# Second q in quarters, heads 7-6 and 5-4 first, then heads 3-0 as one half, and the place of half a V tile

## The chip, the cores and the metric

The kernel runs on one core of one Trainium2 chip. The metric is the device time of one execution in microseconds. It was measured three times for the kernel before: 178.45, 178.59 and 178.68 us, median 178.59 us. One further execution was profiled, and every duration below is from it.

## The reference

Four rows of 512 numbers pass through an attention layer A, a gated layer B, and then through both again with the same weights:

```python
x = x + _A_ref(_layernorm(x), A_k_cache, A_v_cache, A_wq, A_wo)
x = x + _B_ref(_layernorm(x), B_w_gate, B_w_up, B_w_down)
x = x + _A_ref(_layernorm(x), A_k_cache, A_v_cache, A_wq, A_wo)
x = x + _B_ref(_layernorm(x), B_w_gate, B_w_up, B_w_down)
```

In A, q is `x @ wq` (512 x 4096) for 4 rows and 32 heads of 128. The last 2048 positions of the K and V caches are used, in 8 key-value heads, each shared by 4 query heads. Scores are scaled and go through a softmax, the weighted V are multiplied by wo (4096 x 512). B is `(sigmoid(x @ w_gate) * (x @ w_up)) @ w_down` with 1792 hidden columns. All tensors are bf16. K and V of the window are 16 MB each, wq and wo 4 MB each, and the three matrices of B about 1.8 MB each.

## The kernel before, in words

All weights and caches come from HBM by transfers that SP issues (`dma`, line 398) into one SBUF arena of 50 slots of 128 x 2048 bf16 (0.5 MB each). K of all eight heads stays in the first 32 slots, four slots a head; the rest is a pool of pairs of slots. A program of operations is built first (`_Plan.op`), each with what it reads and writes; `_schedule` (line 92) then orders the operations of each engine by estimated times, and `_assign_sync` gives each the semaphore waits that its dependencies need. SP's order is the order of building; after `P.chain = True` TensorE's is too. A transfer whose place is still being read waits on SP, and everything behind it on SP waits as well.

Around the second attention there is too little room, so pieces of the arena are used in halves. `homes` gives the slots to which a half is bound: Y, Z and GA are the places of the V tiles V(7,0), V(7,1) and V(6,0) (head, pair of batches), GB is a free pair, and a number 0 or 1 says which of its two slots. `hfree` lists the ones that are free. `load_glu(0)` puts the first B's weights there, `load_wq(1)` (line 522) the second q's weights: eight transfers of 0.5 MB, first the four of heads 7 to 4 (i = 1), one for each 128 of the 512 inputs, then the four of heads 3 to 0 (i = 0). `load_v` (line 609) loads V(6,0) and V(5,1) of the second attention in halves.

V(7,0) and half of V(7,1) of the first attention are needed again in the second and are not loaded twice. `stash` and `stash_half` transpose them into PSUM banks (0 to 3, and 4 and 5), and they return later: `load_stash` (line 587) writes banks 0 to 3 into a pair from the pool, `unstash_half` (line 603) writes banks 4 and 5 back into slot Z.

The second attention goes through heads 7 to 0 (u = 0 to 7). In `q_second` (line 824) TensorE multiplies heads 7 to 4 into bank 6; VectorE transposes it (`q_turn`, line 803) into `qh`. `q_unit` (line 834) spreads one head of q over a block-diagonal operand, `softmax_unit` (line 861) makes the mask product M and the scores S and then, in `soft`, the maximum and the exponential, `turn_p` transposes the weights, `pv_wide` multiplies by V. `attn_second` (line 1201) writes this order out by hand. When the scores of a head are done, its K slots go to the pool, and `fill` puts the next transfers on SP. The banks of scores are given by the line

```python
bank, pt = {HKV: (OBS[0], 2), HKV + 1: (WB, 3)}.get(u, (SB[k2], k2))
```

so head 7's scores go to bank 4, head 6's to bank 6, later ones to banks 0 and 1.

## Time and profile before

| | |
|---|---|
| median of three runs | 178.59 us |
| profiled execution: its time, its span | 178.86 us, 177.1 us |
| mean granted TensorE clock | 0.944 |
| busy: TensorE products, VectorE, ScalarE | 102.2, 104.4, 32.7 us |
| DMA | 70.52 MB, 12882 packets, mean 398 GB/s |
| V: loads, size, median time to landing | 27 of 1024 KB, 22.6 us, and 3 of 512 KB, 5.6 us |
| second wq: loads, size, median time to landing | 8 of 512 KB, 6.1 us |

The span runs from the first to the last instruction. A share of busy time is an average over stages. The granted clock is 1.0 in each 2 us slice from 92 to 156 us and 0.5 from 158 us on. The time from issue to landing says how deep the DMA queue is when a transfer is put in: 6.1 us around the second q, over 20 us for most others. In the views shown below, a line of the timeline holds start and duration in us, engine, source line and operation, and in brackets how long the engine had been idle and what ended that; a line of the slices holds the stretch, its length, the busy time of the five engines, TensorE's clock, the DMA share and GB/s; a line of the chain holds start, duration and what.

### The profile page before, as it was taken

Reading aid. Unit: us, or ns where it says so; the run is one execution under the profiler, and the core shown is the slowest. Engines: PE = TensorE matmul, PEld = TensorE weight load, DVE = VectorE, ACT = ScalarE, POOL = GpSimd, SP = SyncE. Lnnn points to the kernel's source line nnn. Section 1 sums busy time; section 2 is a strip of 40 time slices with the busy share of each in tenths; the row PEclk is TensorE's granted clock in tenths of the full one; section 3 lists DMA queues with packets and bytes.
Section 4 is the critical chain, followed back from the end, with each engine's and each line's share of the span. In section 5 each row is a group of like instructions: output and inputs, shape, how many; then the busy total and the mean of one; then the engine's idle time right before and its main releaser. Section 6 shows DMA issues by size and latency. Waiting matters only on the chain.

```text
span 177.1 us, 3893 instructions
## 1 busy us (share of the span) xinstructions
PE 102.2 (58%) x1641; PEld 55.0 (31%) x1653; DVE 104.4 (59%) x256; ACT 32.7 (18%) x87; POOL 21.6 (12%) x88
## 2 busy tenths in 40 slices
PE   0536336481842635607417866466986999776664
PEld 0202102241431421603404752052322444435322
DVE  7307997838476374593483772323299999742351
ACT  2002031312030300300201101000043455430011
POOL 6100010101010100100100100000011453342000
PEclk9999999999999999999999999999999999975555
DMA  5999999999999999999999999999999999999980
GB/s 182 425 427 424 429 420 416 407 425 429 411 413 417 425 422 418 407 422 431 413 416 429 401 402 405 401 408 381 407 416 411 420 420 424 418 411 406 413 347 24
DMA packets 12882, 70.52 MB, mean 398 GB/s; under 512 B 1336, under 2 KB 1344, under 8 KB 6720
## 3 DMA queue, kind: packets, MB, share of 16 engines
q1 hardware_dynamic: 12856, 70.26, 97.2%
q8 instruction: 13, 0.21, 0.5%
q14 instruction: 5, 0.04, 0.1%
q10 hardware_dynamic: 8, 0.00, 0.0%
HBM read 70.26 MB, written 0.00 MB: 397 GB/s over the span
## 4 chain that ended last, share of the span: by engine, by line
DMA 38%; DVE 32%; PE 18%; issue 4%; SPq 4%; ACT 3%; DVEq 0%; ACTq 0%
DMA arena<-in_B_w_down_dram 15%; DMA arena<-in_A_v_cache_dram 15%; DVE arena L854 11%; PE ps L883 7%; DVE nmax L896 5%; DMA arena<-in_B_w_gate_dram 4%; DMA arena<-in_A_wq_dram 4%; SPq L398 4%; PE ps L973 3%; PE ps L872 2%; DVE nmax L900 2%; DVE mxt L904 2%; DVE ebuf L931 2%; PE ps L1162 2%; DVE arena L1064 2%
## 5 line engine op out<-in xcount | busy, mean ns | idle before, releaser
L854 DVE STREAM_TRANSPOSE arena<-arena 128x1024 f32<-128x1024 f32 x32 | 37.0, 1202 | 0.0
L883 PE MATMUL ps<-arena,qbd 128*32 128x512 bf16 x256 | 25.5, 534 | 0.0
L896 DVE TENSOR_REDUCE nmax<-ps 128x1 f32<-128x512 f32 x16 | 10.8, 676 | 19.4 <-PE ps L883 19.2
L973 PE MATMUL ps<-ebuf,arena 128*128 128x8 bf16 x576 | 17.8, 168 | 7.6 <-DMA arena<-in_A_v_cache_dram 4.2
L872 PE MATMUL ps<-msk_m,msk_s 128*32 128x512 bf16 x64 | 8.6, 526 | 23.1 <-DVE arena L854 21.8
L973 PEld LDWEIGHTS ps<-ebuf,arena 128*128 128x128 bf16 x576 | 16.8, 104 | 9.6 <-DMA arena<-in_A_v_cache_dram 5.5
L911 ACT ACTIVATE prow<-ps,nmax 128x512 bf16<-128x512 f32 x16 | 11.0, 687 | 35.1 <-DVE nmax L908 29.5
L847 ACT CAST qbd<-ps 128x256 bf16<-128x256 f32 x16 | 5.9, 370 | 44.9 <-PE ps L883 35.0
L940 POOL CAST s<-psm 128x1 bf16<-128x1 f32 x9 | 1.7, 187 | 83.9 <-ACT prow L911 83.9
L883 PEld LDWEIGHTS ps<-arena,qbd 128*32 128x32 bf16 x256 | 8.3, 121 | 10.4 <-issue 7.8
L795 PE MATMUL ps<-arena,xn 128*4 128x512 bf16 x64 | 8.3, 572 | 5.0 <-DMA arena<-in_A_wq_dram 4.5
L926 ACT CAST prow<-ps 128x512 bf16<-128x512 f32 x16 | 9.4, 586 | 9.8 <-PE ps L973 2.1
L1342 PE MATMUL ps<-arena,xn 128*4 128x448 bf16 x64 | 7.8, 548 | 4.1 <-DMA arena<-in_B_w_up_dram 1.9
L931 DVE STREAM_TRANSPOSE ebuf<-prow 128x256 f32<-128x256 f32 x16 | 7.0, 436 | 3.8 <-ACT prow L926 3.7
L872 PEld LDWEIGHTS ps<-msk_m,msk_s 128*32 128x32 bf16 x64 | 1.7, 98 | 24.1 <-DVE arena L854 22.7
L773 ACT ACTIVATE lnv<-ps 128x4 f32<-128x4 f32 x4 | 0.7, 174 | 41.0 <-PE ps L769 41.0
L807 DVE STREAM_TRANSPOSE ebuf<-ps 128x512 f32<-128x512 f32 x3 | 2.1, 717 | 10.2 <-PE ps L795 10.1
L1055 PE MATMUL ps<-arena,ebuf 128*32 128x512 bf16 x112 | 8.0, 409 | 0.2 <-DVE nmax L908 0.2
L842 PE MATMUL ps<-qh,eyew 32*128 32x64 bf16 x64 | 5.6, 217 | 3.8 <-ACT qbd L847 2.4
L1351 DVE STREAM_TRANSPOSE ebuf<-ps 128x448 f32<-128x448 f32 x4 | 2.6, 650 | 7.0 <-PE ps L1342 7.0
L1162 PE MATMUL ps<-onp,arena 128*128 128x16 bf16 x144 | 5.3, 175 | 2.5 <-DVE onp L996 2.2
L981 DVE TENSOR_TENSOR onb<-ps,rinv 128x16 bf16<-128x16 f32 x9 | 1.7, 185 | 8.3 <-PE ps L973 8.1
(112 smaller groups left out, 132.2 us busy)
## 6 DMA issues: line engine op xcount, KB each, us to landing
arena<-in_A_v_cache_dram SPq DMA_DIRECT2D x27, 1024.0 KB, 22.6
arena<-in_A_k_cache_dram SPq DMA_DIRECT2D x16, 1024.0 KB, 25.2
arena<-in_A_wq_dram SPq DMA_DIRECT2D x4, 1024.0 KB, 7.9
arena<-in_A_wq_dram SPq DMA_DIRECT2D x8, 512.0 KB, 6.1
arena<-in_A_wo_dram SPq DMA_DIRECT2D x3, 1024.0 KB, 26.2
arena<-in_B_w_down_dram SPq DMA_DIRECT2D x4, 512.0 KB, 6.3
arena<-in_B_w_gate_dram SPq DMA_DIRECT2D x4, 448.0 KB, 8.4
arena<-in_B_w_up_dram SPq DMA_DIRECT2D x4, 448.0 KB, 6.1
```

The lines of the kernel that those rows point to most:

```text
L795: last = pe.matmul(ps[32 * hh:32 * hh + NB, qb, :], xn[:, c * NB:(c + 1) * NB], src[:, o + hh * 512:o + (hh + 1) * 512], start=(c == 0), s ...
L854: P.op("vector", "T%d_%d" % (h, t), c_dve(1024), lambda v, v32=v32: v.transpose(v32, v32), r=[("slot", 4 * h + t)], w=[("slot", 4 * h + t)])
L872: last = pe.matmul(ps[32 * gi:32 * gi + 32, bank, :], msk_s[:, :], msk_m[:, :].unsqueeze(1).broadcast_to([128, 256, 2]), start=True, stop= ...
L883: last = pe.matmul(ps[32 * gi:32 * gi + 32, bank, :], qbd[:, q0:q0 + 32], kt[:, cp // 2, cp % 2, jh * NJ:(jh + 1) * NJ, :], start=False, s ...
L896: lambda v: v.tensor_reduce(nmax[:, k2:k2 + 1], ps[:, bank, :], AXX, ALU.max),
L911: lambda a: a.activation(prow[:, :].rearrange("p (m x t) -> p m x t", x=32, t=2), ps[:, bank, :].rearrange("p (m t x) -> p m x t", x=32, t ...
L926: P.op("scalar", "pc" + tag, c_act(512), lambda a: a.copy(prow[:, :], ps[:, pb, :]), r=[("ppb", pb)], w=[("prow",)], banks=(pb,))
L931: P.op("vector", "pt" + tag, c_dve(256), lambda v: v.transpose(et, prow[:, :].bitcast(F32)), r=[("prow",)], w=[("e", k2)])
L973: last = pe.matmul(ps[:, ob, bp * 8:bp * 8 + 8], src[:, j * 128:(j + 1) * 128], ev[:, j % 2, j % 16 // 2, x0:x0 + 8], start=(j == 0), stop ...
L1055: last = pe.matmul(ps[32 * g:32 * g + 32, ob, :], ew[:, g, mq, t], src.rearrange("p (m t d) -> p t m d", t=2, d=128)[:, t], start=(n == 0) ...
L1162: last = pe.matmul(ps[:, WB, c * NR:(c + 1) * NR], tile_ap(s)[:, o + r_ * D + c * 128:o + r_ * D + (c + 1) * 128], ov[:, r_ * NR:(r_ + 1) ...
L1342: last = pe.matmul(ps[32 * g:32 * g + NB, gub[n], 0:NF], xn[:, c * NB:(c + 1) * NB], slot_ap(s)[:, g * NF:(g + 1) * NF], start=(c == 0), s ...
```

## The change

The weights of heads 7 to 4 still come in four transfers of 0.5 MB, but each now holds two of the four blocks of 128 inputs and the columns of two heads: 128 partitions of 2 rows of 1024 columns. The pair for heads 7 and 6 comes first (j = 1), then that for heads 5 and 4. `q_pair` multiplies them with 256-wide products, two for each group of columns, into bank 6 and into columns 256 to 511 of bank 7, and `q_pair_turn` transposes each quarter and multiplies by the reciprocal deviation, twice, with a factor that is zero on the rows of the other head (`hide`, two more exponentials). Heads 3 to 0 come last as before, but their second block goes to the first slot of Z, and all four products are made after head 6's scores, into bank 4. Head 7's scores go to bank 6, head 6's to bank 5.

The half tile returns from banks 4 and 5 into the first K slot of head 7 (`base[KA]`), one half before head 7's maximum and one after its `nm`; the second of those slots takes the second half of V(5,1), whose first half goes to Y; V(6,0)'s half goes to GA. The first pair of head 7's K slots therefore reaches the pool later. `load_stash` comes after the third load of V instead of the second. On SP, V(4,0) waits for the third scores of the second attention, where it had waited for the second.

On the engines this makes 16 more products and weight loads on TensorE, six more instructions on VectorE, two more on ScalarE; SP issues the same number of transfers.

```diff
-        msks = sb("msks", [128, 22], F32)
+        msks = sb("msks", [128, 24], F32)
...
-        selm = msks[:, 18:22].bitcast(BF16)
+        selm, hide = msks[:, 18:22].bitcast(BF16), msks[:, 22:24]
...
+        BACK = ("back",)
+        KA = ("first",)
...
             def emit(s):
-                dma(str(name), slot_ap(s)[:, 0:size], src, w=[("slot", s)], rate=rate)
+                dst = slot_ap(s)[:, 0:size]
+                if name[0] == "wqp":
+                    dst = dst.rearrange("p (f n) -> p f n", f=2)
+                dma(str(name), dst, src, w=[("slot", s)], rate=rate)
             loads.append((name, emit))
...
             else:
-                for i in (1, 0):
-                    for c in range(NC):
-                        load_half(("wq", c, k, i), wq_d[:, c, i * SLOT:(i + 1) * SLOT], "bw_4k", SLOT,
-                                  (((Y, 1), (GB, 0), (GB, 1), (GA, 0)), ((GB, 0), (GB, 1), (GA, 0), (Y, 0)))[i][c])
+                for j in (1, 0):
+                    for n in range(2):
+                        o = SLOT + j * (SLOT // 2)
+                        load_half(("wqp", n, j), wq_d[:, 2 * n:2 * n + 2, o:o + SLOT // 2], "bw_4k", SLOT,
+                                  (((GA, 0), (Y, 0)), ((GB, 0), (GB, 1)))[j][n])
+                for c in range(NC):
+                    load_half(("wq", c, k, 0), wq_d[:, c, 0:SLOT], "bw_4k", SLOT, ((Y, 1), (Z, 0), (GB, 0), (GB, 1))[c])
...
 
-        def unstash_half(after):
-            for n in range(2):
-                dst = slot_ap(base[Z])[:, n * 1024:(n + 1) * 1024].bitcast(F32)
+        def unstash_half():
+            where[BACK] = base[KA]
+            left[BACK] = 1
+            halves[HKV - 1, 1] = [(BACK, 0), (Z, 1)]
+            for n in (1, 0):
+                dst = slot_ap(base[KA])[:, n * 1024:(n + 1) * 1024].bitcast(F32)
                 P.op("vector", "uo%d" % n, c_dve(512), lambda v, dst=dst, n=n: v.transpose(dst, ps[:, OBS[n], :]),
-                     r=[("so", n)], w=[("slot", base[Z])], banks=(OBS[n],), after=after)
+                     r=[("so", n)], w=[("slot", base[KA])], banks=(OBS[n],))
 
...
             name = ("V", h, bp, k)
-            tiles = {(HKV - 2, 0): ((Y, 0),), (HKV - 3, 1): ((Y, 1), (GB, 0))}.get((h, bp)) if k else None
+            tiles = {(HKV - 2, 0): ((GA, 0),), (HKV - 3, 1): ((Y, 0), (KA, 1))}.get((h, bp)) if k else None
             if tiles is not None:
...
                     halves[h, bp].append((half, 0))
+                    if tile == (KA, 1):
+                        on_free[half] = lambda s: pool.release(s - 1)
                 if len(tiles) == 1:
...
+        on_free[BACK] = lambda s: None
...
+        P.op("vector", "zero_c", 300.0, lambda v: v.memset(ps[:, CB, 256:512], 0.0), w=[("c0",)], banks=(CB,))
...
+        P.op("vector", "hide", 100.0, lambda v: v.tensor_scalar(hide[:, :], maskb[:, :], 1.0, 1.0e30, ALU.subtract, ALU.mult),
+             r=[("maskb",)], w=[("hide",)])
...
                      r=[("cb",)], w=[("lnv",)], banks=(CB,))
+                if tag == "Q":
+                    for n, (rs, t) in enumerate(((lnd[:, 0:nb], ("lnd",)), (lnr[:, NB:NB + nb], ("lnr", 1)))):
+                        P.op("scalar", "ln_rs%d" % n, c_act(NB),
+                             lambda a, n=n, rs=rs: a.activation(rs, lnv[:, 0:nb], ACTF.Exp, bias=hide[:, n:n + 1], scale=-0.5),
+                             r=[("lnv",), ("hide",)], w=[t])
                 P.op("scalar", "ln_rstd" + tag, c_act(NB),
...
 
+        QP = {1: (WB, 0), 0: (CB, 256)}
+
+        def q_pair(j, n):
+            qb, o = QP[j]
+            name = ("wqp", n, j)
+            s = need(name)
+
+            def e_q(pe):
+                last = None
+                for c in (2 * n, 2 * n + 1):
+                    for g in range(4):
+                        w0 = c % 2 * (SLOT // 2) + g * 256
+                        last = pe.matmul(ps[32 * g:32 * g + NB, qb, o:o + 256], xn[:, c * NB:(c + 1) * NB],
+                                         slot_ap(s)[:, w0:w0 + 256], start=(c == 0), stop=(c == NC - 1), skip_group_check=True)
+                return last
+            P.op("tensor", "qp%d_%d" % (j, n), 6 * tm["pe_row"], e_q, r=[("slot", s), ("xn",)], w=[("qrow", 2 + j)], banks=(qb,))
+            done(name)
+
+        def q_pair_turn(j):
+            qb, o = QP[j]
+            k = 1 - j
+            buf = ebuf[:, k * 256:(k + 1) * 256]
+            fresh.append(P.op("vector", "qpt%d" % j, c_dve(256),
+                              lambda v: v.transpose(buf, ps[:, qb, o:o + 256].rearrange("p (x k t) -> p x t k", k=32, t=2)),
+                              r=[("qrow", 2 + j)], w=[("e", k)], banks=(qb,)))
+            qi = qh[:, k * 64:(k + 1) * 64].rearrange("p (x s r) -> p s x r", s=2, r=2)
+            for n, rs in enumerate((lnd[:, 0:NB], lnr[:, NB:2 * NB])):
+                P.op("vector", "qpc%d_%d" % (j, n), c_dve(32),
+                     lambda v, n=n, rs=rs: v.tensor_tensor(
+                         qi[:, n].rearrange("p (c b) r -> p c b r", c=4),
+                         buf.rearrange("p (r c y) -> p c y r", c=4, y=32)[:, :, 0:NB],
+                         rs.unsqueeze(1).unsqueeze(3).broadcast_to([128, 4, NB, 2]), ALU.mult),
+                     r=[("e", k), (("lnd",), ("lnr", 1))[n]], w=[("qh", k)])
+
         def q_second(variance):
-            q_mms(1, 1, WB, (0, 1))
+            q_pair(1, 0)
             variance()
-            unstash_half(())
-            q_mms(1, 1, WB, (2, 3))
-            q_mms(1, 0, OBS[1], (0,))
-            fresh.append(q_turn(1, 1, WB))
+            q_pair(1, 1)
+            q_pair_turn(1)
+            q_pair(0, 0)
 
...
         def q_unit(tag, h, k2):
-            hh = h % 4
-            src = qh[32 * hh:32 * hh + 32, h // 4 * 64:h // 4 * 64 + 64].rearrange("p (x r) -> p x r", r=REP)
+            p0, np_, k = 32 * (h % 4), 32, h // 4
+            if h >= 4 and tag[0] != "0":
+                p0, np_, k = 64 * (h % 2), 64, 1 - (h - 4) // 2
+            src = qh[p0:p0 + np_, k * 64:k * 64 + 64].rearrange("p (x r) -> p x r", r=REP)
             dst = ps[:, CB, 0:256].rearrange("p (x y) -> p x y", y=NR)
...
                 for a in range(4):
-                    last = pe.matmul(dst[:, :, a * REP:(a + 1) * REP], eyew[32 * hh:32 * hh + 32, 96 - 32 * a:224 - 32 * a],
+                    last = pe.matmul(dst[:, :, a * REP:(a + 1) * REP], eyew[p0:p0 + np_, 96 - 32 * a:224 - 32 * a],
                                      src, start=True, stop=True)
                 return last
-            P.op("tensor", "qx" + tag, 250.0, e_qx, r=[("qh", h // 4), ("eyew",)], w=[("cb",)], banks=(CB,))
+            P.op("tensor", "qx" + tag, 250.0, e_qx, r=[("qh", k), ("eyew",)], w=[("cb",)], banks=(CB,))
             P.op("scalar", "qe" + tag, c_act(256),
...
-            bank, pt = {HKV: (OBS[0], 2), HKV + 1: (WB, 3)}.get(u, (SB[k2], k2))
+            bank, pt = {HKV: (WB, 2), HKV + 1: (OBS[1], 3)}.get(u, (SB[k2], k2))
...
                 if u == 0:
+                    base[KA] = 4 * hs[0]
+                    unstash_half()
                     soft(0)
-                for bp in range(2):
-                    pool.release(4 * hs[u] + 2 * bp)
+                    hfree.add(base[KA] + 1)
+                    named("mx" + tag(0))[0].deps.update(named("uo1"))
+                    named("uo0")[0].deps.update(named("nm" + tag(0)))
+                for bp in range(2 if u else 1):
+                    pool.release(4 * hs[u] + 2 * bp + (0 if u else 2))
                 fill()
...
 
+            def rest_of_pair():
+                q_pair(0, 1)
+                q_pair_turn(0)
+
             qx(0)
-            score(0, lambda: q_mms(1, 0, OBS[1], (1,)))
+            score(0, rest_of_pair)
             qx(1)
...
             qx(2)
+            q_mms(1, 0, OBS[0], (0, 1))
             slots = []
...
                 left[name] += 1
-            q_mms(1, 0, OBS[1], (2, 3))
+            q_mms(1, 0, OBS[0], (2, 3))
             wide_buffers(slots, P.ops[-1])
...
             sum_up(0)
-            q_turn(1, 0, OBS[1], rest["tv", 1], [("tv", 1)], [o for o in P.ops if o.name == "pt2.0"])
+            q_turn(1, 0, OBS[0], rest["tv", 1], [("tv", 1)], [o for o in P.ops if o.name == "pt2.0"])
             soft(1)
...
                     n_v += 1
-                    if n_v == cfg.get("ST", 2):
+                    if n_v == cfg.get("ST", 3):
                         load_stash(("V",) + keep[0] + (1,))
...
```

## The prediction, as made before the changed kernel ran

> **What bounds the kernel now.** I read the page first: the slices, the queues, then the chain of waits around the second q and at the end.
>
> ```profile
> DMA  5999999999999999999999999999999999999980
> GB/s 182 425 427 424 429 420 416 407 425 429 411 413 417 425 422 418 407 422 431 413 416 429 401 402 405 401 408 381 407 416 411 420 420 424 418 411 406 413 347 24
> ...
> q1 hardware_dynamic: 12856, 70.26, 97.2%
> q8 instruction: 13, 0.21, 0.5%
> ```
>
> The DMA engines are busy from the second slice to the last but one, and the kernel's own queue q1 takes 97.2% of 16 engines' span. No compute engine is above 59%. The tail of the chain says the same:
>
> ```profile
> 152.83 20.84 DMA arena<-in_B_w_down_dram
> 173.71 0.60 PE ps L1383 x16
> 174.34 0.41 PE ps L1383 x5
> 174.78 0.28 DVE ebuf L1394
> 175.06 0.32 DVEq L1496
> ```
>
> A transfer issued at 152.83 lands 20.84 us later, so the queue is some 20 us deep there, and everything behind the last landing (174.30 by its landing signals) is a tail of 177.1 - 174.30 = 2.8 us. The span is therefore the queue's time plus a tail that the change does not touch.
>
> The change works at 113 to 134 us. Slices of 2 us over it show one dip:
>
> ```profile
> 118.00:120.00 2.00, 1.11 (x14) 0.91 (x14) 1.41 (x6) 0.00 (x0) 0.00 (x0) 1.00 1.04 406
> 120.00:122.00 2.00, 1.70 (x14) 0.68 (x10) 0.80 (x2) 0.17 (x1) 0.00 (x0) 1.00 1.01 406
> 122.00:124.00 2.00, 1.06 (x8) 0.09 (x4) 0.21 (x1) 0.20 (x1) 0.00 (x0) 1.00 1.04 352
> 124.00:126.00 2.00, 1.58 (x16) 0.64 (x20) 0.77 (x2) 0.37 (x1) 0.00 (x0) 1.00 1.02 408
> ```
>
> The last column is GB/s: 352 at 122 to 124 against 406. Its cause is in the issue times: q's transfers leave at 113.01, 114.14, 115.79, 116.71, 118.01, and the sixth only at 120.49, since its place (the pair's first slot) is read by q until then. The gap is 2.48 us where 0.5 MB takes 1.27 us.
>
> Who loses by that dip decides the case. Each transfer signals its landing 16 times, once for each DMA engine. The fifth q transfer landed between 122.49 and 124.34, the sixth between 124.47 and 125.60: the first engine lost 1.98 - 1.27 = 0.71 us, the last engine 125.60 - 124.34 = 1.26, nothing. TensorE, which waits for the last of the 16, shows it too:
>
> ```profile
> 121.86 0.09 PEld L795 LDWEIGHTS ps<-arena,xn 128*4 128x4 bf16 x4 [0.24 <-DMA arena<-in_A_wq_dram]
> ...
> 123.14 0.09 PEld L795 LDWEIGHTS ps<-arena,xn 128*4 128x4 bf16 x4 [1.19 <-DMA arena<-in_A_wq_dram]
> ...
> 124.38 0.09 PEld L795 LDWEIGHTS ps<-arena,xn 128*4 128x4 bf16 x4 [1.15 <-DMA arena<-in_A_wq_dram]
> ...
> 125.65 0.09 PEld L795 LDWEIGHTS ps<-arena,xn 128*4 128x4 bf16 x4 [0.22 <-DMA arena<-in_A_wq_dram]
> ```
>
> The loads follow at 1.28, 1.24, 1.27 us, straight through the dip. So the slowest engines never ran dry.
>
> Why are some slow? The instruction queue q8 moved 13 blocks in 0.5% of 16 x 177.1 us, 1.1 us each, and each holds one DMA engine for that time: at 134.52 the last signal of one transfer, at 138.22 that of the next (1 MB, normally 2.48), 3.70, just after a block at 133.7. In the last transfer eight engines are done by 172.43, four by 172.84, four at 173.90 to 174.30: three groups, as if by no, one and two blocks. Eight engines had been made late by the eight blocks before 120; the four blocks from 133.7 to 164.1 each moved an engine that was already among the latest. The end is set by engines hit twice, and these were not the ones that ran dry at 122.
>
> **The change, part by part.**
> *Bytes.* The same 4 MB of q weights, the same V. But q's heads 7 to 4 now come as four transfers of 256 rows of 2 KB instead of four of 128 rows of 4 KB. The price is in the trace, in the waits of w_down's load, whose last transfer has 2 KB rows:
>
> ```profile
> 116.09 0.50 PEld L1408 LDWEIGHTS ps<-hT,arena 128*128 128x128 bf16 x16 [0.42 <-DMA arena<-in_B_w_down_dram]
> ...
> 117.38 0.51 PEld L1408 LDWEIGHTS ps<-hT,arena 128*128 128x128 bf16 x16 [0.79 <-DMA arena<-in_B_w_down_dram]
> ...
> 118.05 0.29 PEld L1408 LDWEIGHTS ps<-hT,arena 128*128 128x128 bf16 x8 [0.16 <-DMA arena<-in_B_w_down_dram]
> ```
>
> 0.25 MB in 2 KB rows takes 118.05 - 117.38 = 0.67, against half of 1.27 = 0.635. The packet records agree: median 84 ns for 2 KB, 159 for 4 KB; 16 x 84 - 8 x 159 = 72 ns for each engine and transfer. Four transfers: 4 x 0.072 = 0.29 us on every engine, the latest too. Bounds: 0.28 by the waits, 0.32 by wo's halves (0.67 and 0.68), 0 if the rows somehow overlap better; I take 0.29.
> (The Trainium skill, "DMA: Bandwidth & Descriptors", section "Why small descriptors are slow (HBM only)", gives a fixed 3 cycles beside a descriptor's 32-byte beats. By that, an estimate, two of 2 KB cost 134 cycles against 131, some 0.03 us a transfer and 0.12 in all; the measured rows say more than twice that, and no row here shows the cycles. The sum by the page would be 178.7.)
>
> *Issue times.* Second q transfer of heads 3-0 goes to slot Z, whose tile V(7,1) now returns to head 7's K slots, and so waits for w_down's last product (about 118.5) instead of q (120.49). The next two wait for the first quarter's two products. Their landings become 119.28 + 0.07 = 119.35 and 120.70; eight 256-wide products stream the columns of four 512-wide ones, so about 0.64: issues at about 120.5 and 121.3, before 121.23 and 122.51. The hole goes, and with it up to 0.7 us of the early engines' loss. On the path of the latest engines this is worth 0.
>
> *TensorE, VectorE, ScalarE.* Added: 16 products with their weight loads; two quarter transposes and four short multiplies for one transpose and one multiply (0.72 and 0.26 now); two exponentials of 0.2; a clear of 256 columns and one small mask at the start. The start is covered: q's second weights land at 8.13, the fourth at 13.19, and TensorE waits 1.47 us for that. The unstash pair (2 x 0.71) leaves 118.8 to 120.8 and goes round head 7's softmax. Scores of head 7 start after the fourth quarter transfer (123.10 + 0.29 = 123.39, plus 0.64) at 124.1 and end at 126.0 (1.92), now 128.1. Then uo1 0.71, the softmax steps 1.6, uo0 0.71, the four unstash transposes 2.47: 131.5, now 132.10. From there VectorE's chain runs on as before, 0.6 us earlier. Worth 0 at the end, since V lands at the queue's rate; it adds to the 0.48 us by which TensorE waits for the last w_up load at 169.98.
>
> *What is queued on SP behind new waits.* The half V into slot 29 and V(5,0) wait for head 7's scores (126.0); V(4,0) now waits for the third scores instead of the second, about 132.9 instead of 131.12, with all later V behind it. From issue to first data took 2.7 (120.49 to 124.47 - 1.27) to 3.1 us (108.53 to 112.88 - 1.27). The latest engine wants the half V at 131.0, so issue by 127.9, 1.9 spare; it wants V(4,0) at about 138.5, so by 135.4, 2.5 spare. Cost 0; without that cover every microsecond late is one on the end.
>
> Sum against the profiled span: 177.1 + 0.29 + 0 = 177.4. The profiled execution took 178.86, the median of three is 178.59; the same shift puts the median at **178.9**.
>
> **The rivals.**
> *Faster.* The engines that set the end do run dry at 122, because my three groups are inferred from landing signals without an engine's name. For it: the page's 352 GB/s and the tidy gap of issues. Against: the latest signals pass at 1.26. Price: at most 0.71 back, less 0.29: 178.2.
> *Slower: SP runs dry behind the scores.* The third scores need all four stash banks returned, which now stand behind uo1, the first softmax and uo0. If V(4,0) left after 135.4, all engines would starve; at 136.4, with the 0.29, the time is 179.9. For it: one V less stands in the queue between the second and third scores. Against: 2.5 us to spare by rows.
> *Slower: instruction blocks.* TensorE runs 32 instructions more, so blocks come 32 instructions earlier. The block at 173.56 moves to about 172.7 and could hold an engine that is still loading. On one of the last four: +1.1 and 0.29, 180.0; on the group of 172.84 it would be hidden (172.84 + 0.29 + 1.1 = 174.2 below 174.59). (The Trainium skill, "Runtime: NRT & Kernel Launch", section "Instruction fetch mechanics", has blocks of 256 instructions and calls the crossing mostly hidden; here a block costs one DMA engine 1.1 us, so for a kernel bound by DMA the trace does not agree.)
> *It does not do what it says:* the hole stays, because two transfers still wait for q. Then the same 0.29, nothing else: the same time.
>
> **How the numbers follow.** Forecast, with the hole gone or not: 0.60, own range 178.6 (a small q14 instruction block, 0.3, falls off the latest engine) to 179.1. Faster rival 0.20, spread 177.9 to 178.5; late SP 0.10; block on a late engine 0.06; others 0.04. The range 178.0 to 179.4 leaves out the low tail of the faster case (0.04) and most of the slower ones (0.14). 0.2% is 0.36 us, about what a measurement can tell: same runs from 178.23 to 178.95. The forecast case gives same 0.40, slower 0.20; the faster one faster 0.14, same 0.06; the rest slower 0.15, faster 0.05. Together: faster 0.19, same 0.46, slower 0.35.
>
> **What would show it.** Right: q's sixth transfer issued near 118.5, no slice under 395 GB/s from 118 to 130, head 7's maximum at about 126.8 instead of 128.12, yet the last w_down landing at about 174.6 with the gap between the first and the last engine wider than 2.5 us. Wrong: the last landing before 174.0 (the early engines mattered), a slice under 380 GB/s at 132 to 140 (SP starved), or 13 or more blocks with one on the last four engines after 165.

## The result, and the profile after

The changed kernel took 179.80 us, median of nine runs (178.91 to 180.54); the kernel before, run beside it, 178.60 us (178.45 to 178.74). The ratio is 1.0066, with a 95% interval of 1.0042 to 1.0090: slower by 1.2 us. The forecast was 178.9, within 178.0 to 179.4; the time lies above that range. What also differs is the scatter: 1.6 us between the fastest and the slowest of these runs, where the kernel before has 0.3. (In the later sessions five of 77 runs of the kernel before came to 179.3 to 181.0 too, and two more, at 181.5, are counted as slow and left out.) The profiled execution took 180.22 us; its span is 178.5.

The page of the changed kernel, the slices (40 equal parts of the span) and the queues:

```profile
GB/s 188 426 426 426 424 419 415 415 424 420 420 411 424 419 420 422 412 421 420 419 420 424 397 403 407 408 385 406 407 421 329 408 415 428 420 416 401 418 304 15
DMA packets 13394, 70.52 MB, mean 395 GB/s; under 512 B 1336, under 2 KB 1344, under 8 KB 7232
...
q1 hardware_dynamic: 13368, 70.26, 96.6%
q8 instruction: 13, 0.21, 0.5%
```

Before, the dip was in the 28th slice (381); now the 28th has 406 and the 31st has 329. The 512 additional packets are the 2 KB rows. There are still 13 instruction blocks. The slices of 2 us of the changed kernel show it more closely (last two columns: DMA share and GB/s):

```profile
118.00:120.00 2.00, 1.17 (x18) 0.81 (x17) 0.91 (x6) 0.00 (x0) 0.00 (x0) 1.00 1.05 384
120.00:122.00 2.00, 1.42 (x22) 0.69 (x18) 0.56 (x3) 0.75 (x4) 0.00 (x0) 1.00 1.06 394
122.00:124.00 2.00, 2.00 (x28) 0.81 (x29) 0.32 (x2) 0.37 (x1) 0.00 (x0) 1.00 1.04 409
124.00:126.00 2.00, 2.00 (x24) 0.55 (x12) 1.05 (x4) 0.00 (x0) 0.00 (x0) 1.00 1.02 406
...
134.00:136.00 2.00, 1.71 (x26) 0.78 (x22) 1.06 (x6) 0.37 (x1) 0.29 (x1) 1.00 0.84 340
136.00:138.00 2.00, 1.56 (x29) 0.50 (x25) 1.87 (x6) 1.36 (x3) 0.31 (x1) 1.00 1.00 311
138.00:140.00 2.00, 1.81 (x34) 0.82 (x26) 1.90 (x8) 0.79 (x3) 0.98 (x2) 1.00 0.99 377
```

Three things are to be read here. At 118 to 122 the rate is 384 and 394 with a DMA share above 1: the engines are busy and move fewer bytes a second, which is what 2 KB rows look like. The hole at 122 is gone, 409 for 352. And at 134 to 140 there is a new one, wider and deeper: 340, 311, 377, where the kernel before has 406, 422, 422.

The issue times say where it comes from. V(4,1) left SP at 128.93 and V(4,0) only at 134.69, a gap of 5.76 us after which everything else follows. V(4,0) waits for the third scores. TensorE's rows there, of the changed kernel (start, duration, line, and the number of products):

```profile
130.63 1.88 PE L817 MATMUL ps<-arena,xn 128*4 128x512 bf16 x16
132.72 1.92 PE L940 MATMUL ps<-arena,qbd 128*32 128x512 bf16 x16
```

and the same work in the kernel before:

```profile
131.11 0.60 PE L795 MATMUL ps<-arena,xn 128*4 128x512 bf16 x8
...
132.38 1.08 PE L883 MATMUL ps<-arena,qbd 128*32 128x512 bf16 x16
```

Line 817 is the second q of heads 3 to 0, now all sixteen products instead of eight between the second and the third scores; line 940 (883 before) is the third scores. The sixteen products of the scores take 1.92 us instead of 1.08. The column of the granted clock shows 1.00 in all these slices, but for the earlier ones that is no measurement: the trace's first clock record begins at 135.00 us in the changed kernel and at 130.04 in the kernel before (full clock from there), and a slice without a record is shown as 1.00. By the durations TensorE ran at half speed until then; the last section has the figures. So the third scores met the half clock after the change and the full clock before it.

The end of the chain of waits of the changed kernel has the same form as before, one late landing:

```profile
130.71 1.80 PE ps L817 x9
132.94 1.71 PE ps L940 x8
...
153.40 21.64 DMA arena<-in_B_w_down_dram
```

but q's products and the third scores now stand in it, and the last landing is at 175.67, where it was 174.30. That is 1.37 us of the 1.4 by which the span grew; the tail is 2.8 us as before.

### The profile page after: what moved, and what is told of

Read it like the earlier page. It is cut to its first block, busy times and chain, and to the rows that moved or that the text cites. A ratio compares the mean times of both kernels' runs of the same rounds, so it can differ in the third digit from the quotient of the medians.

```text
span 178.5 us, 3946 instructions
## 1 busy us (share of the span) xinstructions
PE 107.8 (60%) x1669; PEld 55.7 (31%) x1669; DVE 105.9 (59%) x262; ACT 33.1 (19%) x89; POOL 21.7 (12%) x88
## 4 chain that ended last, share of the span: by engine, by line
DMA 43%; DVE 27%; PE 20%; SPq 3%; issue 3%; ACT 2%; DVEq 0%; ACTq 0%
DMA arena<-in_A_v_cache_dram 24%; DMA arena<-in_B_w_down_dram 12%; DVE arena L911 9%; PE ps L940 8%; DVE nmax L953 4%; DMA arena<-in_A_wq_dram 4%; DMA arena<-in_B_w_up_dram 3%; SPq L398 3%; PE ps L929 3%; PE ps L1030 2%; DVE nmax L957 2%; PE ps L981 2%; DVE arena L1121 2%; DVE ebuf L988 2%; DVE mxt L961 2%
## 5 line engine op out<-in xcount | busy, mean ns | idle before, releaser
L940 PE MATMUL ps<-arena,qbd 128*32 128x512 bf16 x256 | 26.7, 554 | 0.0
L981 PE MATMUL ps<-prow,perm 128*128 128x512 bf16 x16 | 8.1, 508 | 8.4 <-ACT prow L968 7.5
L817 PE MATMUL ps<-arena,xn 128*4 128x512 bf16 x48 | 6.0, 609 | 2.9 <-DMA arena<-in_A_wq_dram 2.9
L1112 PE MATMUL ps<-arena,ebuf 128*32 128x512 bf16 x112 | 7.4, 384 | 0.2 <-DVE nmax L965 0.2
L899 PE MATMUL ps<-qh,eyew 32*128 32x64 bf16 (+1 forms) x64 | 5.7, 221 | 3.0 <-ACT qbd L904 2.4
```

The source lines that it names most:

```text
L817: last = pe.matmul(ps[32 * hh:32 * hh + NB, qb, :], xn[:, c * NB:(c + 1) * NB], src[:, o + hh * 512:o + (hh + 1) * 512], start=(c == 0), s ...
L940: last = pe.matmul(ps[32 * gi:32 * gi + 32, bank, :], qbd[:, q0:q0 + 32], kt[:, cp // 2, cp % 2, jh * NJ:(jh + 1) * NJ, :], start=False, s ...
L981: lambda pe: pe.matmul(ps[:, pb, :], perm[:, :], prow[:, :], start=True, stop=True),
L1112: last = pe.matmul(ps[32 * g:32 * g + 32, ob, :], ew[:, g, mq, t], src.rearrange("p (m t d) -> p t m d", t=2, d=128)[:, t], start=(n == 0) ...
```

## The experiments

Each was timed in 6 to 12 runs beside the kernel before, except the last one, which is a single run. The kernel before had medians of 178.61, 178.64 and 178.66 us in the three sessions.

**V(4,0) in two halves (e2).** The changed kernel, but V(4,0) goes into two half slots that are idle by then, so it needs no slot of the third scores.

```diff
-            tiles = {(HKV - 2, 0): ((GA, 0),), (HKV - 3, 1): ((Y, 0), (KA, 1))}.get((h, bp)) if k else None
+            tiles = {(HKV - 2, 0): ((GA, 0),), (HKV - 3, 1): ((Y, 0), (KA, 1)), (HKV - 4, 0): ((Y, 1), (Z, 0))}.get((h, bp)) if k else None
...
+                    if tile == (Z, 0):
+                        on_free[half] = lambda s: pool.release(s)
...
+        on_free[Z] = lambda s: None
```

> The changed kernel, with V(4,0) of the second attention loaded in two halves into the two halves that stand idle after q (the second slot of Y and the first of Z), so that it leaves after the products of heads 3-0 (about 131.1 and 131.5 us) instead of after the third scores (134.69). Theory A (the queue runs dry at 134 to 138 us because V(4,0) comes late): no slice under 390 GB/s from 134 to 140, last w_down landing near 174.6, median 178.6 + 0.29 (2 KB rows) + 0.05 (4 KB instead of 8 KB rows for 1 MB) = 178.9, and the scatter of the runs falls to that of the kernel before. Rival B (the quarters themselves cost it: 2 KB rows, 16 more products, later instruction blocks): stays at 179.5 to 180. Rival C (the early engines' loss at 122 us mattered, and only the new dry stretch hid the gain): 178.2 to 178.4.

Measured: 179.01 us (178.79 to 179.28), ratio 1.0015 [0.9992, 1.0037]. The halves left at 130.43 and 131.01. The slices of 2 us of this version:

```profile
134.00:136.00 2.00, 1.24 (x24) 0.52 (x21) 1.87 (x6) 1.34 (x4) 0.31 (x1) 1.00 1.04 418
136.00:138.00 2.00, 1.81 (x34) 0.88 (x26) 1.90 (x8) 0.75 (x4) 0.97 (x2) 1.00 0.98 399
138.00:140.00 2.00, 2.00 (x31) 0.65 (x23) 1.83 (x7) 0.99 (x4) 0.56 (x2) 1.00 1.05 430
```

The new dip is gone, and with it 0.8 us and the scatter, as theory A had it. What is left is 0.4 us above the kernel before.

**The wait alone, in the kernel before (e3).** The first pair of head 7's K slots is held back until the third head's V products, and the stash is loaded third, as in the change; nothing else of the change is in it.

```diff
-                for bp in range(2):
-                    pool.release(4 * hs[u] + 2 * bp)
+                for bp in range(2 if u else 1):
+                    pool.release(4 * hs[u] + 2 * bp + (0 if u else 2))
...
                 pv_wide(tag(u), hs[u], u % 2, v_tiles[(2, hs[u])])
+                if u == 2:
+                    pool.release(4 * hs[0])
+                    fill()
...
-                    if n_v == cfg.get("ST", 2):
+                    if n_v == cfg.get("ST", 3):
```

> The kernel before, with one part of the change alone: the first pair of head 7's K slots goes to the pool only after the third head's V products, and the stash returns after the third V load; q as before. V(4,0) then waits for the third scores (about 134.3 us instead of 131.12). Theory A: the queue runs dry around 135 to 138, a slice under 370 GB/s, median 179.1 to 179.8, and runs that scatter by more than 0.5 us. Rival B (the quarters cost it): 178.6, like before.

Measured: 179.51 us (178.60 to 180.68), ratio 1.0044 [1.0016, 1.0072]. V(4,0) left at 133.76, and the slices of 2 us have the dip a little later:

```profile
136.00:138.00 2.00, 1.42 (x22) 0.70 (x23) 1.84 (x7) 0.79 (x3) 0.47 (x2) 1.00 1.01 397
138.00:140.00 2.00, 1.81 (x29) 0.83 (x32) 1.87 (x10) 1.09 (x4) 1.38 (x4) 1.00 0.80 279
140.00:142.00 2.00, 2.00 (x36) 0.96 (x38) 1.90 (x6) 0.79 (x3) 0.52 (x2) 1.00 1.01 369
```

So the held pair makes the loss (+0.9) and the scatter by itself, without quarters and without 2 KB rows, as theory A said (the hold and the later stash were put in together, so the run doesn't part them). One thing in this trace doesn't fit the simple picture: V(4,0) itself landed 2.42 us behind V(4,1) on the first engine, on time, and the dry stretch came one transfer later, before V(3,1), which SP had issued at 134.34 and which the first engine finished 3.23 us after V(4,0) (the last 2.67). Why that transfer came late is not explained; in e7 below, with the same two issue times, it came after 2.47.

**A larger hole at 122 (e4, e5).** The kernel before, with the places of q's transfers exchanged so that the sixth waits for one or two more products.

```diff
-                                  (((Y, 1), (GB, 0), (GB, 1), (GA, 0)), ((GB, 0), (GB, 1), (GA, 0), (Y, 0)))[i][c])
+                                  (((Y, 1), (GB, 1), (GB, 0), (GA, 0)), ((GB, 0), (GB, 1), (GA, 0), (Y, 0)))[i][c])
...
-            tiles = {(HKV - 2, 0): ((Y, 0),), (HKV - 3, 1): ((Y, 1), (GB, 0))}.get((h, bp)) if k else None
+            tiles = {(HKV - 2, 0): ((Y, 0),), (HKV - 3, 1): ((Y, 1), (GB, 1))}.get((h, bp)) if k else None
```

(e5 has `(Y, 1), (GA, 0), (GB, 0), (GB, 1)` in the first line and `(GA, 0)` in the second.)

> The kernel before, with the places of the second and third q transfers of heads 3-0 exchanged (and the half of V(5,1) that follows there), so that the sixth q transfer waits for the second product of q: issue about 121.2 instead of 120.49, a gap of 3.2 us instead of 2.5 to the fifth. The early engines run dry 0.7 us longer, the latest still have work (their last data at 124.3, first new data about 123.9 to 124.3). Theory A (only engines that instruction blocks hit late count): 178.6 within 0.2. Rival C (every dry microsecond of any engine counts): 178.9 to 179.3.

> The same with the sixth q transfer waiting for the third product of q: issue about 122.5, a gap of 4.5 us. Now the latest engines run dry too, from 124.3 to about 125.2. Theory A: the last landing moves by what the latest engines lose, 0.8 to 1.2 us: 179.4 to 179.8. If the kernel stays at 178.6, something else than the DMA queue sets its end.

Measured: e4 179.06 us (178.75 to 179.45), ratio 1.0013 [0.9991, 1.0036], sixth transfer at 121.03; e5 180.27 us (179.94 to 180.83), ratio 1.0087 [1.0063, 1.0112], sixth transfer at 122.75. e4 costs about 0.45, although its latest engine went almost straight through (124.12 to 125.44, 1.32 for 1.27 us) and lost only 0.3 at the transfer behind the next; e5's latest engine lost 1.7 in all, and the time is 1.66 longer. Theory A's figures were too low for both, by some 0.3 to 0.5, but not its rule: by what the latest engine did lose, 0.4 and 1.7, the rule fits both runs. The average over the sixteen landings, 0.4 and 1.9 us more than in the kernel before at these transfers, fits about as well. So these two runs don't tell the rules apart.

**The 2 KB rows doubled (e6).** The halves version with q of heads 3 to 0 in 2 KB rows too; the products read the columns from the two slots.

```diff
-                    load_half(("wq", c, k, 0), wq_d[:, c, 0:SLOT], "bw_4k", SLOT, ((Y, 1), (Z, 0), (GB, 0), (GB, 1))[c])
+                    n, o = c // 2 * 2, c % 2 * (SLOT // 2)
+                    load_half(("wq", c, k, 0), wq_d[:, n:n + 2, o:o + SLOT // 2], "bw_4k", SLOT, ((Y, 1), (Z, 0), (GB, 0), (GB, 1))[c])
```

> The version with V(4,0) in halves (179.01 us), and in addition the four q transfers of heads 3-0 in rows of 2 KB, two for each partition (rows of two blocks of inputs, columns of two heads), in the same places; the products of blocks 0 and 1 wait for two transfers instead of one, and are made together anyway. Theory A (a transfer of 0.5 MB in 2 KB rows costs every engine 0.07 us more): four more such transfers, +0.29, 179.3 (179.15 to 179.5); landings of the last four q transfers 1.33 to 1.36 us apart. Rival B (the rows cost nothing at the end, the 0.4 us of the halves version over the kernel before come from something else): 179.0 as before, at most 179.1.

Measured: 179.36 us (179.27 to 179.52), ratio 1.0038 [1.0026, 1.0050]: 0.35 above the halves version for four more such transfers, or 0.09 each. Its last four q transfers landed 1.34 to 1.35 us apart. In the slices of 2 us the share is full and the rate stays below 400 until 128, where the halves version is back at 408 by 122:

```profile
120.00:122.00 2.00, 1.43 (x22) 0.65 (x18) 0.56 (x3) 0.75 (x4) 0.00 (x0) 1.00 1.05 389
122.00:124.00 2.00, 2.00 (x28) 0.83 (x32) 0.37 (x2) 0.37 (x1) 0.00 (x0) 1.00 1.06 390
...
126.00:128.00 2.00, 1.50 (x18) 0.59 (x20) 1.83 (x6) 0.37 (x1) 0.00 (x0) 1.00 1.05 394
```

**4 KB rows with the new places (e10).** The halves version, with the whole-width transfers of the kernel before for heads 7 to 4.

```diff
-                for j in (1, 0):
-                    for n in range(2):
...
+                for c in range(NC):
+                    load_half(("wq", c, k, 1), wq_d[:, c, SLOT:2 * SLOT], "bw_4k", SLOT, ((GB, 0), (GB, 1), (GA, 0), (Y, 0))[c])
...
-            q_pair(1, 0)
+            q_mms(1, 1, WB, (0, 1))
             variance()
-            q_pair(1, 1)
-            q_pair_turn(1)
-            q_pair(0, 0)
+            q_mms(1, 1, WB, (2, 3))
+            fresh.append(q_turn(1, 1, WB))
...
-            score(0, rest_of_pair)
+            score(0)
```

> The version with V(4,0) in halves, but q of heads 7 to 4 in the four transfers, rows of 4 KB and products of the kernel before, with the places of the changed kernel kept (no hole at 122, nothing waits for the third scores but V(3,1)). Head 7's scores come about 2 us later again. Theory A (rows cost 0.29, closing the hole gains nothing): 0.29 below 179.01, so 178.7 (178.5 to 178.85), the time of the kernel before. Rival B (the rows cost nothing): 179.0. Rival C (closing the hole gains up to 0.7 and the rows hid it): 178.0 to 178.4.

Measured: 179.94 us (179.43 to 180.82), ratio 1.0071 [1.0046, 1.0095]. None of the three expectations. The slices of 2 us tell what they had left out:

```profile
128.00:130.00 2.00, 1.50 (x16) 0.60 (x20) 1.83 (x5) 0.37 (x1) 0.00 (x0) 1.00 0.85 317
130.00:132.00 2.00, 1.13 (x12) 0.16 (x4) 1.87 (x5) 0.78 (x2) 0.00 (x0) 1.00 0.96 326
...
136.00:138.00 2.00, 1.70 (x26) 0.59 (x18) 1.17 (x5) 0.27 (x1) 0.29 (x1) 1.00 0.99 291
```

The second half of V(5,1) lives in head 7's K slots and waits for head 7's scores, here 2 us later: it left at 128.03 instead of 125.63, and the queue ran dry at 128 to 132. V(4,1) then left at 131.17 instead of 127.77, and 136 has a dip too. So the run doesn't price the rows. What it shows is that the new places lean on the quarters: without head 7's scores 2 us earlier they cost 0.9 or more.

**The hole put back (e8).** The halves version with the second and third transfers of heads 3 to 0 exchanged; blocks 0 and 2 are multiplied first.

```diff
-                    load_half(("wq", c, k, 0), wq_d[:, c, 0:SLOT], "bw_4k", SLOT, ((Y, 1), (Z, 0), (GB, 0), (GB, 1))[c])
+                    load_half(("wq", c, k, 0), wq_d[:, c, 0:SLOT], "bw_4k", SLOT, ((Y, 1), (GB, 0), (Z, 0), (GB, 1))[c])
...
-            q_mms(1, 0, OBS[0], (0, 1))
+            q_mms(1, 0, OBS[0], (0, 2))
...
-            for c in (NC - 2, NC - 1):
+            for c in (1, 3):
...
-            q_mms(1, 0, OBS[0], (2, 3))
+            q_mms(1, 0, OBS[0], (1, 3))
```

> The version with V(4,0) in halves, with the second q transfer of heads 3-0 put back behind the first quarter's products (places of the second and third exchanged; blocks 0 and 2 are multiplied first, then 1 and 3, since two slots must stay). The hole opens again: sixth q transfer issued at about 120.4 instead of 118.3, the slice at 122 near 350 GB/s. Theory A (the engines that run dry there don't set the end): 179.0 (178.85 to 179.2). Rival C (they do): 0.4 to 0.7 more, 179.4 to 179.7.

Measured: 179.23 us (178.75 to 179.83), ratio 1.0031 [1.0016, 1.0045], which overlaps the interval of the halves version. The sixth transfer left at 120.40 as meant, but its first engine lost only 0.07 us (122.88 to 124.22) and the slice at 122 has 381, not 350: the 2 KB rows ahead of it had put every landing 0.4 us later, and so filled most of the hole. The run is no clean test; the hole as it was left here is worth between nothing and 0.4.

**The third scores ahead of q's products (e7).** The changed kernel, with its V(4,0).

```diff
+            score(2)
             q_mms(1, 0, OBS[0], (0, 1))
...
             wide_buffers(slots, P.ops[-1])
-            score(2)
```

> The changed kernel with V(4,0) as it is, but the sixteen q products of heads 3-0 moved behind the third scores on TensorE. The third scores then start when the four stash banks have returned, 131.5 instead of 132.30, and V(4,0) leaves at 132.8 to 133.3 instead of 134.69, near the 132.9 that the prediction had. Theory A (the engines' lead that is lost in the dry stretch decides, so each part of it counts in part): 179.2 (179.0 to 179.4), V(4,0)'s first engine lands 0 to 0.4 us later than the queue's rate, scatter of the runs mostly gone. Rival B (any V(4,0) behind the third scores costs as much, whatever the issue time): 179.6 to 179.9 with the scatter kept. Rival D (TensorE's slow products in the third scores cost by themselves): the same 179.6 to 179.9, but with V(4,0) landing on time.

Measured: 179.07 us (178.80 to 180.76), ratio 1.0046 [1.0020, 1.0072]. The runs fall into two groups, seven at 178.80 to 179.08 and five at 180.10 to 180.76, and the profiled one, 180.21 us, is of the longer group. In it V(4,0) left at 133.77. Its first engine lost 0.36 us (135.43 to 138.27 for 2.48), its last nothing, and the last landing is at 174.25, as early as in the kernel before. What made this execution long is not the queue: the tail behind the last landing is 4.1 us instead of 2.8. One row of TensorE and two of the chain of waits:

```profile
131.80 1.92 PE L940 MATMUL ps<-arena,qbd 128*32 128x512 bf16 x16
...
140.44 1.71 PE ps L940 x15
...
175.03 0.98 PE ps L1450 x56
```

The trace records a granted clock of one half from 129.52 to 143.18 us, and sixteen products take 1.9 us all through that stretch. At the end all 56 products of w_down run at 175.03, when their weights have landed, and wait for VectorE instead of a transfer. So here the engines, not the data, end last; that the half clock brought it about is argued from this one trace. The median is 0.7 below the changed kernel's, but with two groups of runs and a trace of the longer one, this can't be put down to the issue time; and the scatter stays, as against theory A.

**More work ahead of the third scores (e9).** The changed kernel with eight more q products, whose results the real ones overwrite.

```diff
+            P.op("tensor", "more", 8 * tm["pe_row"], e_more, r=[("slot", where["wq", 0, 1, 0]), ("xn",)],
+                 w=[("qrow", 0)], banks=(OBS[0],))
             q_mms(1, 0, OBS[0], (0, 1))
```

> The changed kernel with eight more products of q's first block in front of the sixteen q products of heads 3-0 (the same products, overwritten by the real ones). They take 0.9 to 1.0 us on TensorE ahead of the third scores, so V(4,0) leaves at 135.5 to 135.8 instead of 134.69. Theory A (what counts is when V(4,0) is issued, each engine losing what it waits beyond its own lead): the last engine now loses some 0.5 us itself and the first 2.5, 180.2 to 180.9, and together with the run that brought the scores forward (V(4,0) at 133.77, 179.07) and the changed kernel (134.69, 179.8) a curve that steepens. Rival B (the loss of the changed kernel comes from chance positions of the instruction blocks, not from the issue time): 179.6 to 179.9. The prediction's own rule (nothing until 135.4, then microsecond for microsecond): 0.1 to 0.4 above the changed kernel.

Measured: 179.46 us (178.86 to 180.72), ratio 1.0045 [1.0017, 1.0072]. All three expectations took for granted that more products mean a later V(4,0). It left at 134.53, 0.16 earlier than in the changed kernel. TensorE's rows of this kernel:

```profile
130.82 1.02 PE L1312 MATMUL ps<-arena,xn 128*4 128x512 bf16 x8
131.63 1.71 PE L817 MATMUL ps<-arena,xn 128*4 128x512 bf16 x16
...
133.39 1.11 PE L940 MATMUL ps<-arena,qbd 128*32 128x512 bf16 x16
```

and its slices, with the granted clock third from the right:

```profile
130.00:132.00 2.00, 1.50 (x16) 0.66 (x21) 1.95 (x4) 0.86 (x2) 0.00 (x0) 0.50 1.05 430
132.00:134.00 2.00, 2.00 (x32) 0.84 (x28) 0.60 (x1) 0.00 (x0) 0.57 (x3) 0.75 1.02 418
134.00:136.00 2.00, 1.52 (x30) 0.69 (x22) 1.83 (x9) 0.37 (x1) 0.42 (x2) 1.00 0.95 360
136.00:138.00 2.00, 1.24 (x28) 0.55 (x21) 1.87 (x6) 1.36 (x3) 0.30 (x1) 1.00 0.90 348
```

The trace records full clock from 126.16 to 129.57 us, half clock to 132.99 and full clock from there. The q products run at half speed, and the scores at the full one: 1.11 us for the 1.92 of the changed kernel. What the additional products cost, the clock gave back. The full clock of 126.16 came before the additional products ran, so they are not what made this execution's clock differ from the changed kernel's. The run doesn't test the issue time, then, but finds what moves it.

**The changed kernel once more (e11).**

> The changed kernel once more, for a second trace and one time, since its runs lie from 178.9 to 180.5. Theory A (engines that lose their lead in the dry stretch, and are then hit or not hit by a later instruction block): V(4,0) issued at 134.7 again within 0.2, third scores about 1.9 us again, the first engine 1.6 late again, and a last landing that differs from 175.67 by which engines the later blocks hit. Rival B (the issue time itself varies between executions): V(4,0) issued earlier by 0.5 or more in a shorter run.

Measured: 179.69 us in one run. V(4,0) left at 134.78; the third scores took 1.92 us again. The first engine lost 1.49 us, the last 0.22 (138.53 to 141.23), and the last landing is at 175.13, 0.54 before that of the first profile. So the issue time was within 0.1 in two executions half a microsecond apart, which speaks for theory A. Rival B is not excluded by two executions: in both the full clock came late, at 135.00 and 135.24.

## Why the prediction was wrong

**What held.** The price of the 2 KB rows: 0.29 predicted for four transfers; four more of them measured 0.35, and the landings in the changed kernel were 1.33 to 1.36 us apart instead of 1.27. (The estimate from the Trainium skill, "DMA: Bandwidth & Descriptors", "Why small descriptors are slow (HBM only)", 0.12 for four, is too small by three times.) The hole at 122 was closed: sixth transfer at 118.30, no dip. Head 7's maximum came at 126.54 (126.8 predicted), the four transposes that return the stash ended at 131.45 (131.5). That closing the hole gains nothing agrees with the halves version, whose 0.40 above the kernel before is the rows' 0.35 and 0.05 more; the hole was not removed without the rows, so a gain of some 0.2 that other parts of the change ate up is not excluded.

**The step that failed** is the one on V(4,0): "about 132.9 instead of 131.12 ... by 135.4, 2.5 spare. Cost 0". The issue time was wrong, and so was the way the spare time was counted.

*The issue time was mis-sized by 1.8 us, by TensorE's speed.* After the stash was back at 131.45, two things stood ahead of the third scores that the sum didn't have. The sixteen q products of heads 3 to 0 ran from 130.63 to 132.5, so the scores began at 132.72 and not at about 131.8, 0.95 us later; that all four products come after head 6's scores is plain in the change, but the sum had them on no path. And the scores took 1.92 us where 1.08 had been read from the trace of before, 0.84 more. 0.95 + 0.84 is the difference from 132.9 to 134.69. Both come of the half clock before 135.00. In e2's trace, where TensorE has the same order and the full clock came at 125.35, the same two rows are

```profile
130.00 1.03 PE L820 MATMUL ps<-arena,xn 128*4 128x512 bf16 x16
...
131.40 1.08 PE L943 MATMUL ps<-arena,qbd 128*32 128x512 bf16 x16
```

There the q products are done by 131.03, no later than the stash (131.12), and V(3,1), which waits for the third scores in that version, left at 132.53. So at full speed the prediction's 132.9 comes out. What it left out is that this stretch can run at half speed; its own rows had 1.92 us for head 7's scores and 1.08 for the third, and it took each to belong to its place. No trace of the changed kernel has the full clock so early, so what V(4,0) costs when it leaves at 132.5 isn't shown.

*The spare time was counted at the wrong engine.* By the prediction's own rule 134.69 was still before 135.4 and should have cost nothing, and the latest engine indeed lost nothing: V(4,1)'s last signal was at 138.42 and V(4,0)'s at 140.90, 2.48 us as in a full queue. But the first engine lost 1.64 us (135.24 to 139.36 is 4.12), and the others values between. (The first engine means the first of the sixteen signals here, whichever engine it is of; an average over the sixteen doesn't depend on that.) The signals of the two transfers, of the changed kernel, and of the two after them:

```
issued 128.93  landed 135.24 135.46 135.58 135.61 ... 137.10 137.41 138.42
issued 134.69  landed 139.36 139.40 139.44 139.48 ... 140.48 140.89 140.90
issued 135.27  landed 141.90 141.91 142.02 142.05 ... 142.96 143.36 143.41
issued 136.56  landed 144.43 144.49 144.54 144.55 ... 145.45 145.84 145.91
```

Before the dry stretch the engines stand 3.2 us apart, after it 1.5. The lead that the early engines had is gone, and three more instruction blocks (145.0, 153.7 and 163.8) of some 1.0 to 1.1 us each, and small ones, are still to come before the last transfers. In the kernel before, the blocks at 153.0 and 164.1 left the last signals 2.46 and 2.25 us apart, as without a block. Now two of three make a new latest engine: behind the block at 145.04, and a small one at 146.32, the last signal goes from 145.91 to 149.10, 3.19 us for one transfer; behind the one at 163.8 from 163.90 to 166.79, 2.89 where 2.26 is usual; behind the one at 153.7 the step is 2.55. Read so, a lead is not idle capacity but what the queue pays its later blocks with. The chain from lead to block is read from the traces of the changed kernel and argued from there: the landing signals don't name their engine, and no run removed a block.

What the sixteen engines lost on average at V(4,0), beyond the 2.48 us of a full queue, grows with its issue time: 0.20 us in e7 (133.77), 0.54 in e9 (134.53), 0.92 in the changed kernel (134.69) and 1.08 in e11 (134.78). All of these lie before 135.4.

Whether such a loss reaches the end can be followed to the last transfer. The table gives the bytes that the slices miss against the reference and the same as time, at the queue's 0.42 MB a microsecond; then how much later the sixteen landings of the last transfer are on average, how much later the latest of them is, and the times.

| kernel, against | missing | as time | last transfer, mean | latest | profiled execution | medians |
|---|---|---|---|---|---|---|
| e4, before (122 to 128) | 0.20 MB | 0.5 us | 0.15 us | 0.0 us | 0.0 us | 0.45 us |
| e5, before (122 to 130) | 0.83 MB | 2.0 us | 1.77 us | 1.66 us | 1.66 us | 1.66 us |
| e3, before (136 to 142) | 0.45 MB | 1.1 us | 0.87 us | 0.46 us | 0.54 us | 0.90 us |
| changed kernel, e2 (134 to 140) | 0.44 MB | 1.0 us | 0.95 us | 1.31 us | 1.21 us | 0.79 us |
| e11, e2 (134 to 140) | 0.50 MB | 1.2 us | 1.12 us | 0.77 us | 0.68 us | one run |
| e7, e2 (134 to 142) | 0.25 MB | 0.6 us | 0.42 us | -0.1 us | 1.20 us | 0.06 us |
| e9, e2 (134 to 140) | 0.28 MB | 0.7 us | 0.60 us | 0.1 us | 0.06 us | 0.45 us |

The mean of the last sixteen landings comes back at 0.1 to 0.3 us less than the missing time in every row, and in e9, the changed kernel and e11 it is what was lost on average at V(4,0) (0.60 for 0.54, 0.95 for 0.92, 1.12 for 1.08). The time of the same execution does not: it goes with the latest landing (all but e7, where the tail is longer), and that stands 1.07 to 2.07 us behind the mean, 2.07 and 1.36 in the two executions of the changed kernel. So e4 and e9 lost bytes and, in the executions that were profiled, no time (the kernel before's was itself 0.25 us above its median). The medians of e4, e3, the changed kernel and e9 lie nearer to the mean than to the latest; in e5 both lost about the same, and e7's trace is of the longer group. This points to the mean over the engines as what to price, with a scatter on top by how far the latest engine happens to stand behind it; with one profile for each kernel it is a rule of thumb and no law.

**The rivals.** "SP runs dry behind the scores" was the right mechanism, at 0.10 and 179.9, almost the measured time, but with a decision point (135.4) that the kernel never reached. "Faster, because the dry engines at 122 matter" had the sign wrong; its rule, that the engines ahead count too, is borne out by the new hole, where the latest lost nothing, while e4 and e5 fit it and the prediction's rule alike. "Instruction blocks" as it was put, a 13th block moved to 172.7, didn't happen: the last block is at 174.9. "The hole stays" was wrong.

**In sum:** 0.35 of the 1.2 us is the rows and 0.8 the place of half a V tile, which holds back 1 MB of head 7's K slots and so puts V(4,0) behind the third scores, which TensorE made at half speed in both traces. The closing of the hole and the earlier scores give nothing that these runs can see.

**Open:** why the late transfer in e3's trace was V(3,1) and not V(4,0). And why a single run lies at 178.9 or at 180.5. The kernels in which V(4,0) hangs on the third scores scatter by 1.6 to 2.1 us (e3, e7, e9, the changed one) and the halves version by 0.5; but e8 and e10, which have V(4,0) in halves too, scatter by 1.1 and 1.4. Three causes were seen that can differ between executions: the engines that later blocks fall on, the time from which TensorE has its full clock, which moves V(4,0), and a half clock in the second attention as in e7's trace. Which of them makes a given run fast was not settled. No version here has a lower median than the kernel before.

## What to carry over

In a queue that is always full, a late transfer is not free because the latest engine still has work: here the latest lost nothing, and the loss that stayed to the end was about what all engines lost on average. When a transfer's wait is moved from one instruction to another, walk the new one's engine from its last known time, with everything that the change itself has put in front of it, and at both of the speeds that the trace shows for such work. A clock column may show 1.00 where the trace has no clock record; the durations of like products tell. And where runs fall into two groups, see which group the trace is from before it is set beside a median. A place that is freed later is a wait of SP's, and the whole queue stands behind it.

## What the hardware showed beyond that

TensorE had two speeds, and the clock records in the traces tell them apart where the column of the slices does not. Groups of sixteen 512-wide products took 1.08 to 1.12 us or 1.92 us in the same stretch of different kernels, and a time between only where a record of full clock begins inside the group (1.64 for head 6 in the kernel before, from 128.85 to 130.49, with the record from 130.04). In all twelve traces, groups of four 512-wide products that follow one another begin 0.21 to 0.24 us apart inside a record of full clock, and 0.38 us or more, mostly 0.43, within a record of half clock and at any time before the first record; only three groups, at the end of a record, lie between. So the 1.00 that the slices show before the first record, from 92 us on in the kernel before too, is the half speed.

When the full clock comes differs between executions. TensorE's work up to 126 us is the same in seven traces, and the first record of full clock begins at 125.35, 126.11 and 126.16 in e2, e7 and e9, and at 134.00 to 135.24 in e6, the changed kernel, e8 and e11. Within a trace the records last whole multiples of 3.41 us (3.41 to 30.72), the last one excepted. In e9 and e7 the clock fell to 0.50 at 129.57 and 129.52, in e9 while TensorE was idle for 2.24 us. (The Trainium skill, "TensorE: Matmul & The Clock Gate", section "What's actually happening", describes a clock that is halved until a free-running window of 3.4 us has seen enough activity, and under "Seeing it yourself" warns that the recorded clock events are not to be trusted. The two speeds and the lengths of the records agree with the first; the warning is not borne out here, where the records, as far as they go, agree with the products.) So a duration on TensorE between idle stretches is one of two values a factor of 1.8 apart, and the same kernel can meet either; in e9 eight more products in front of a group made it no later.
